# Who issues the paced loads of a backward pass: SyncE for all, or GpSimd for those of the filling products

## The chip, the cores and the metric

The kernel runs on one core of a Trainium2 chip. The metric is the device time of one execution in microseconds, the median over several runs. The core has five engines that run their own instruction streams and wait for each other through semaphores: PE (TensorE, matrix products into PSUM), ACT (ScalarE), DVE (VectorE), POOL (GpSimd) and SP (SyncE, which in this kernel only issues DMAs). PE's weight loads are shown as PEld. A DMA is issued by an instruction in the stream of one engine; an engine works through its stream in order, so a DMA behind a waiting instruction is issued late.

## The reference, cut to what matters

One transformer block in which attention and a gated feed-forward network stand side by side, and its gradients:

```python
def forward(x, wqkv, wo, w_gate, w_up, w_down):      # x: 1 x 2048 x 448, bf16
    xn = layernorm(x)
    q, k, v = split(xn @ wqkv)                         # 16 heads of 28
    p = softmax(q @ k.T * 28 ** -0.5)                  # 2048 x 2048 per head
    attn = (p @ v) @ wo
    ffn = (silu(xn @ w_gate) * (xn @ w_up)) @ w_down   # inner size 1792
    return x + attn + ffn

out, vjp = jax.vjp(forward, x, wqkv, wo, w_gate, w_up, w_down)
return out, *vjp(grad_out)
```

The kernel returns the output and six gradients.

## The kernel before, in words

Heads are worked on in 4 groups `g` of 4 heads. The first part computes the projections, the forward attention and the whole of the feed-forward network's inner work, and leaves in DRAM what the second part needs: queries with their gradients (`QD_d`), keys and values (`KD_d`), the inner activations and their gradients (`F_d`), the attention outputs (`OT_d`), transposed weights (`wT_d`, `wqc_d`).

The second part, the backward pass of attention, is one loop over 512 steps `k` (the constant `NB`), ordered group, head pair `hp`, key block `kc` of 512 keys, query block `qc`, query tile `qi` of 128. In the order of the code a step does the following.

- `row(k)`: PE computes the scores of two heads (line 845) and, for the step before, the gradients of the probabilities (line 853).
- `ew(k)`: ACT takes the exponentials (line 870, tile `e_sb`); DVE multiplies them with the gradients (line 878). The result `ds` goes to a tile `ds_sb` for query tiles 0 to 2 and to `ds_pe` for tile 3.
- For query tiles 0 to 2 of each block `b` of four steps, `dst_dma` lets SP issue a DMA transpose of `ds` into the tile `dsT` (line 863); for tile 3, and for tile 2 of a few blocks, PE transposes and ACT copies (`tr_unit`, lines 938 and 943).
- `kv(k)`: PE sums the gradients of keys and values (lines 956 and 960).
- `dq_unit(b)` comes in step `4 * b + 13`: PE multiplies the `dsT` of the block's four tiles with the keys (line 987), ACT writes the scaled result to `dq_st` (line 1000), which has a single buffer, and POOL adds it to `dq_acc` (line 1002), or for the last key block writes the sum to `dqT` (line 1004).

PE, ACT and DVE keep this order. What is left of PE's time is given to filling products, in pieces, within the steps: `y_unit` (the output, from `h_c`, `o_c`, `x_c`, `wd_e`, `wd_sb`, `wo_sb`; line 1111), `dx_unit` (the feed-forward part of the input's gradient, from `dau_c` and `wguT`; line 1167) and `dc_unit` (the attention part, from `dc` and `wqT`; line 1214), with smaller ones between them. Their order is a list; what each gets in a step is a time budget in the code.

Their operands come from DRAM by paced loads. `drip` puts a load on the list `slow`, sorted by the step in which it is due. In each step `drop` computes a rate that has every load on the list issued three steps before it is due, adds it to a credit, and issues loads from the head of the list while the credit is positive (line 802). `have` issues at once what a unit is about to need and what is still on the list. The keys `kd` and queries `qd` of the next group come by the same list (`load_k`, `load_q`). All of these loads are issued by SP, in the order of the code, between the transposes of `ds`. Results are stored through `store`, which holds each back two steps and then lets POOL issue it (line 835).

Of the kernel before, what the change touches and what calls it, by code (L numbers as in the profile page):

```python
# [105 lines left out]
def kernel(  # L106
# [23 lines left out]
    PE, DVE, ACTE, POOL, SP = nc.tensor, nc.vector, nc.scalar, nc.gpsimd, nc.sync  # L130
# [6 lines left out]
    QD_d = dram.tile([G, 4, P, 4, 512], BF16)  # L137
    KD_d = dram.tile([G, 4, P, 3, 512], BF16)
# [436 lines left out]
    for i in range(len(chain) + LEAD):  # L575
# [4 lines left out]
        k = i - LEAD  # L580
# [102 lines left out]
    for t in range(4):  # L683
        run(T_unit(xnT, xn_t, t, t % 2 == 0, ps_s if t < 2 else None))
    DVE.tensor_reduce(out=r_ones[:],
                      in_=ident_f[:].rearrange("p (a b) -> p a b", b=HP)[:, :, 28:30],
# [11 lines left out]
    for c in range(3):  # L698
        k = 4 * c
        t = 4 * c + 4  # L700
# [37 lines left out]
    def new_q(g, qc):  # L738
        qside[g, qc] = kq.tile([P, 4, 512], BF16, name="qd", bufs=6)
        return qside[g, qc]  # L740

    def new_k(g, kc):
        kside[g, kc] = kq.tile([P, 3, 512], BF16, name="kd", bufs=5)
        return kside[g, kc]
# [29 lines left out]
    slow = []  # L774
    RATE = 100 << 10
    now = 0

    def drip(key, pieces, due):
        slow.extend((due, key, o, i) for o, i in pieces)
        slow.sort(key=lambda x: x[0])  # L780
# [3 lines left out]
    def size(o):  # L784
        nb = 2 if o.dtype == BF16 else 4
        for x in o.shape:
            nb *= x
        return nb

    def drop():  # L790
        nonlocal credit
        if not slow:
            credit = 0
            return
        rate, cum = RATE, 0
        for due, _, o, _ in slow:
            cum += size(o)
            rate = max(rate, (cum - credit) / max(due - now - 3, 1))
        credit += rate
        while slow and credit > 0:  # L800
            _, _, o, i = slow.pop(0)
            SP.dma_start(out=o, in_=i)
            credit -= size(o)

    def have(*keys):
        for x in [x for x in slow if x[1] in keys]:
            slow.remove(x)
            SP.dma_start(out=x[2], in_=x[3])

    def load_q(g, qc):  # L810
        t = new_q(g, qc)
        drip(("q", g, qc), [(t[:], QD_d[g, qc])], 128 * g + 4 * qc - 4)

    def load_k(g, kc):
        t = new_k(g, kc)
        drip(("k", g, kc), [(t[:], KD_d[g, kc])], 128 * g + 16 * kc - 4)

    steps = [(g, hp, kc, qc, qi) for g in range(G) for hp in range(2) for kc in range(4)
             for qc in range(4) for qi in range(4)]
    NB = len(steps)  # L820
# [16 lines left out]
    def row(k):  # L837

        if k < NB:
            g, hp, kc, qc, qi = steps[k]  # L840
            have(("q", g, qc), ("k", g, kc))
            for j in range(2):
                s_ps = ps_b.tile([P, 512], FP32, name="sb", bufs=3)
                r = HP * (2 * hp + j)
                PE.matmul(s_ps[:], lhsT=qside[g, qc][r:r + HP, 0, qi * P:(qi + 1) * P],  # L845
                          rhs=kside[g, kc][r:r + HP, 0, :], start=True, stop=True, tile_position=(r, 0))
                sps[k, j] = s_ps
        if 1 <= k <= NB:
            g, hp, kc, qc, qi = steps[k - 1]
            for j in range(2):  # L850
                d_ps = ps_b.tile([P, 512], FP32, name="db", bufs=3)
                r = HP * pv(2 * hp + j)
                PE.matmul(d_ps[:], lhsT=qside[g, qc][r:r + HP, 1, qi * P:(qi + 1) * P],  # L853
                          rhs=kside[g, kc][r:r + HP, 1, :], start=True, stop=True, tile_position=(r, 0))
                dps[k - 1, j] = d_ps
# [35 lines left out]
    k = 0  # L891
# [200 lines left out]
    load_y(0, 0)  # L1092
    drip(("y", 0, 0), [(wo_sb[:], wo_d[:])], 36)
    load_k(0, 2)
    drip(("y", 0, 1), [(wdp[1][:, a:b, :], wd_v[:, NH + a:NH + b, :]) for a, b in ((0, 4), (4, 7))], 50)

    load_y(0, 1)
    load_k(0, 3)

    def y_unit(ch, half, ti):  # L1100
        if ti == 0:
            have(("y", ch, half))
            nxt = 2 * ch + half + 2
            if nxt < 8:
                load_y(nxt // 2, nxt % 2)
        tsl = slice(ti * P, (ti + 1) * P)
        mm = [(ych[ch, half][:, i, tsl], wdp[half][:, i, :]) for i in range(NH)]
        mm += [(ych[ch, 3 + half][:, i, tsl], wo_sb[:, 2 * half + i, :]) for i in range(2)]
        ps = ps_g.tile([P, 512], FP32, name="genb")
        for i, (l, r) in enumerate(mm):  # L1110
            PE.matmul(ps[:, :D], lhsT=l, rhs=r, start=(i == 0), stop=(i == len(mm) - 1))
            if i < len(mm) - 1:
                yield 189
        if half == 0:
            yts[ti] = yp.tile([P, D], FP32, name="yt", bufs=5)
            DVE.tensor_tensor(out=yts[ti][:], in0=ps[:, :D], in1=ych[ch, 2][:, ti, :], op=ALU.add)
        else:
            y = yp.tile([P, D], BF16, name="y")
            DVE.tensor_tensor(out=y[:], in0=ps[:, :D], in1=yts[ti][:], op=ALU.add)
            store(out0_d[:, 4 * ch + ti, :], y[:])  # L1120
        yield 189
# [33 lines left out]
    def dx_unit(ch, fq, ti):  # L1155
        if ti == 0:
            have(("dx", ch, fq))
            nxt = 4 * fq + ch + 1
            if nxt < 12:
                load_dx(nxt % 4, nxt // 4)  # L1160
        d = dxs[ch, fq]
        f0, f1 = FQ[fq]
        n = 2 * (f1 - f0)
        tsl = slice(ti * P, (ti + 1) * P)
        ps = ps_g.tile([P, 512], FP32, name="genb")
        for i in range(n):
            PE.matmul(ps[:, :D], lhsT=d[:, i // 2, i % 2, tsl], rhs=dxs["w", fq][:, i // 2, i % 2, :],  # L1167
                      start=(i == 0), stop=(i == n - 1))
            if i < n - 1:
                yield 189  # L1170
        o = dxs["g"][:, 4 * ch + ti, :]
        if fq == 0:
            ACTE.copy(out=o, in_=ps[:, :D])
        else:
            DVE.tensor_tensor(out=o, in0=ps[:, :D], in1=o, op=ALU.add)
        yield 189
# [178 lines left out]
    for k in range(NB + 12):  # L1355
        now = k
        if k < NB:
            g, hp, kc, qc, qi = steps[k]
            if hp == 1 and kc > 0 and qc == 2 and qi == 2 and g + 1 < G:
                load_k(g + 1, kc - 1)  # L1360
            if g > 0 and hp == 0 and kc == 0 and qc == 2 and qi == 2:
                load_k(g, 3)
            if hp == 1 and g + 1 < G and qi == 3 and (kc, qc) in NEXT:
                load_q(g + 1, NEXT.index((kc, qc)))
        m = k % 4
        if k <= NB:
            if k >= K0:
                row(k)
                ew(k)
            flush(k)  # L1370
            if 2 <= k:
                drop()
# [89 lines left out]
```

## Time and profile before

| | us |
|---|---|
| median of 3 runs | 1411.97 |
| lowest and highest run | 1410.12, 1415.71 |
| the profiled execution: time | 1411.65 |
| the profiled execution: span, first to last instruction | 1409.9 |
| busy: PE, ACT, DVE, POOL | 1322.0, 1213.3, 1148.3, 411.9 |
| mean granted TensorE clock | 0.981 of full |

The profile is one execution. Busy time of an engine is the union of its instructions; SP has no busy time in it, since issuing is not counted, but its instructions have start and duration in the timeline. "Idle before" is the time that an engine stood still before an instruction, with the instruction or DMA that ended it. The first exponential of the loop of 512 steps starts at 604.1 us and the last step's at 1361, so that a step takes 1.48 us on average and a block of four steps 5.9 us.

### The profile page before, as it was taken

The numbers are of one execution on the slowest core, as the hardware profiler recorded it, in microseconds if no ns is written. First come the engines' busy times: TensorE is split into PE (matmuls) and PEld (weight loads), VectorE is DVE, ScalarE is ACT, GpSimd is POOL, SyncE is SP. The second block draws the span as 40 slices with busy tenths as digits, with TensorE's granted clock in tenths as the row PEclk, the third lists the DMA queues.
The fourth block names the chain that finished last, engine by engine and source line by source line (L and its number), as shares of the span: only waits on it lengthen the run. The fifth ranks groups of instructions, "written<-read, shape, count | busy, mean of one in ns | idle before, by whom it ended". The sixth has DMA issues, their size and how long they took to land. (4 is left out here: it accounts for less than half of the span.)

```text
span 1409.9 us, 34764 instructions
## 1 busy us (share of the span) xinstructions
PE 1322.0 (94%) x12697; PEld 561.2 (40%) x12758; DVE 1148.3 (81%) x2001; ACT 1213.3 (86%) x2199; POOL 411.9 (29%) x577
## 2 busy tenths in 40 slices
PE   5889999989999999988999999999999999999985
PEld 2333333333333333333434444444444444444442
DVE  6577756666666677677989989988899999999988
ACT  5789998989999999867988889899989898888964
POOL 6574534464334444311121111301211112020105
PEclk9899999999999999989999999999999999999998
DMA  6697967876677677699999999999999999999972
GB/s 157 160 206 167 236 138 167 199 157 165 151 193 175 162 168 162 174 234 213 213 223 222 229 222 184 213 222 230 244 170 201 215 218 238 183 182 197 207 144 61
DMA packets 672205, 267.88 MB, mean 190 GB/s; under 512 B 597914, under 2 KB 646546, under 8 KB 672034
## 3 DMA queue, kind: packets, MB, share of 16 engines
q1 hardware_dynamic: 663586, 252.42, 87.9%
q0 software_dynamic: 7040, 12.93, 3.7%
q8 instruction: 100, 1.64, 0.5%
q14 instruction: 71, 0.58, 0.1%
q10 hardware_dynamic: 1408, 0.30, 0.1%
HBM read 64.37 MB, written 59.62 MB: 88 GB/s over the span
## 5 line engine op out<-in xcount | busy, mean ns | idle before, releaser
L870 ACT ACTIVATE e_sb<-sb 128x512 bf16<-128x512 f32 x1024 | 541.1, 606 | 31.4 <-PE db L853 28.3
L878 DVE TENSOR_TENSOR ds_sb<-db,e_sb 128x512 bf16<-128x512 f32 x770 | 483.2, 682 | 33.0 <-issue 9.0
L639 ACT ACTIVATE eT<-s_w 128x1024 bf16<-128x1024 f32 x256 | 264.5, 1033 | 56.0 <-PE s_ps L636 53.7
L641 ACT ACTIVATE eT<-s_ps 128x512 bf16<-128x512 f32 x512 | 286.7, 612 | 0.0
L845 PE MATMUL sb<-kd,qd 32*128 32x512 bf16 x1024 | 234.2, 385 | 5.7 <-DMA kd<-KD_d 2.0
L853 PE MATMUL db<-kd,qd 32*128 32x512 bf16 x1024 | 234.5, 386 | 4.4 <-DVE ds_sb L878 3.7
L1002 POOL TENSOR_TENSOR dq_acc<-dq_acc,dq_st 128x256 f32<-128x256 f32 x64 | 46.2, 723 | 485.2 <-ACT dq_st L1000 485.2
L878 DVE TENSOR_TENSOR ds_pe<-db,e_sb 128x512 bf16<-128x512 f32 x254 | 163.4, 685 | 21.1 <-PE db L853 13.2
L404 POOL TENSOR_TENSOR nn<-nn,ag 128x512 f32<-128x512 f32 x56 | 71.4, 1274 | 242.8 <-DVE ag L402 234.2
L956 PE MATMUL acc<-e_sb,qd 128*32 128x512 bf16 x1024 | 135.6, 387 | 0.0
L636 PE MATMUL s_ps<-QQ,KK 32*128 32x512 bf16 x512 | 120.1, 387 | 2.2
L1167 PE MATMUL genb<-wguT,dau_c 128*128 128x448 bf16 x448 | 109.7, 356 | 0.0
L960 PE MATMUL acc<-ds_sb,qd 128*32 128x512 bf16 x770 | 107.7, 388 | 0.0
L636 PE MATMUL s_w<-QQ,KK 32*128 32x512 bf16 x512 | 100.7, 390 | 3.8 <-ACT eT L639 1.2
L845 PEld LDWEIGHTS <-qd 32*128 32x128 bf16 x1024 | 48.4, 91 | 133.8 <-issue 114.6
L445 PE MATMUL gen<-xn_t,f_sp 128*128 128x448 bf16 x416 | 91.8, 354 | 3.4 <-DVE nn L419 1.9
L943 ACT COPY dsT<-sb 128x512 f32<-128x512 f32 x137 | 79.9, 590 | 16.3 <-PE sb L938 8.2
L445 PEld LDWEIGHTS <-f_sp 128*128 128x128 bf16 x640 | 55.8, 98 | 79.5 <-issue 34.2
L987 PE MATMUL sb<-dsT,kd 128*32 128x256 bf16 x2048 | 79.0, 274 | 6.8 <-DMA dsT<-ds_sb 6.1
L938 PE MATMUL sb<-ident_bf,ds_pe 128*128 128x128 bf16 x1016 | 77.6, 219 | 1.1 <-DVE dsT L941 0.8
L938 PEld LDWEIGHTS <-ds_pe 128*128 128x128 bf16 x1016 | 66.3, 98 | 24.2 <-issue 7.4
L405 POOL TENSOR_TENSOR nn<-nn,tt 128x512 f32<-128x512 f32 x56 | 72.5, 1295 | 4.4
(183 smaller groups left out, 2044.3 us busy)
## 6 DMA issues: line engine op xcount, KB each, us to landing
F_d<-hda SPq DMA_DIRECT2D x56, 384.0 KB
dau_c<-F_d SPq DMA_DIRECT2D x24, 512.0 KB
qd<-QD_d SPq DMA_DIRECT2D x16, 512.0 KB
kd<-KD_d SPq DMA_DIRECT2D x16, 384.0 KB
dsT<-ds_sb SPq DMA_TRANSPOSE x374
h_c<-F_d SPq DMA_DIRECT2D x8, 512.0 KB
wT_d<-wT_f SPq DMA_DIRECT2D x14, 256.0 KB
KD_d<-qk_sp SPq DMA_DIRECT2D x7, 512.0 KB
```

What stands on the lines that cost most here:

```text
L445: PE.matmul(ps[:, :D], lhsT=fsp[fc][:, t // 4, w, t % 4, :], rhs=rhs[:, t, :], start=(t == 0), stop=(t == NT - 1))
L636: PE.matmul(sp4[hh], lhsT=KK[g][r:r + HP, kt * P:(kt + 1) * P], rhs=QQ[g][r:r + HP, qsl], start=True, stop=True, tile_position=(r, 0))
L639: ACTE.activation(out=e2[0][:], in_=wide[:], func=ACT.Exp, scale=SCALE)
L641: ACTE.activation(out=e2[1][:, j], in_=sp4[2 + j], func=ACT.Exp, scale=SCALE)
L845: PE.matmul(s_ps[:], lhsT=qside[g, qc][r:r + HP, 0, qi * P:(qi + 1) * P], rhs=kside[g, kc][r:r + HP, 0, :], start=True, stop=True, tile_po ...
L853: PE.matmul(d_ps[:], lhsT=qside[g, qc][r:r + HP, 1, qi * P:(qi + 1) * P], rhs=kside[g, kc][r:r + HP, 1, :], start=True, stop=True, tile_po ...
L870: ACTE.activation(out=est[k][:, j], in_=sps.pop((k, j))[:], func=ACT.Exp, scale=SCALE)
L878: DVE.tensor_tensor(out=ds[:, j], in0=dps.pop((k - 1, j))[:], in1=est[k - 1][:, j], op=ALU.mult)
L938: PE.transpose(ps[:, c, :], ds[:, c // 4, (c % 4) * P:(c % 4 + 1) * P], ident_bf[:])
L956: PE.matmul(a[r:r + HP, :], lhsT=sp4[:, 1, r:r + HP], rhs=e[:, j, :], start=first, stop=last, tile_position=(0, r), skip_group_check=True)
L960: PE.matmul(a[r:r + HP, :], lhsT=sp4[:, 0, r:r + HP], rhs=ds[:, j, :], start=first, stop=last, tile_position=(0, r), skip_group_check=True)
L1167: PE.matmul(ps[:, :D], lhsT=d[:, i // 2, i % 2, tsl], rhs=dxs["w", fq][:, i // 2, i % 2, :], start=(i == 0), stop=(i == n - 1))
```

## The change

In the loop of 512 steps, POOL issues the paced loads that feed the filling products. SP keeps the loads of keys and queries, and everything that is issued after the last step (`now >= NB`). Keys and queries are put on the list as due eight steps before their first use, where it was four. The list, its pacing and the loads themselves stay.

```diff
+    def by(key):
+        return SP if key[0] in "qk" or now >= NB else POOL
+
     def drop():
...
         while slow and credit > 0:
-            _, _, o, i = slow.pop(0)
-            SP.dma_start(out=o, in_=i)
+            _, key, o, i = slow.pop(0)
+            by(key).dma_start(out=o, in_=i)
             credit -= size(o)
 
     def have(*keys):
         for x in [x for x in slow if x[1] in keys]:
             slow.remove(x)
-            SP.dma_start(out=x[2], in_=x[3])
+            by(x[1]).dma_start(out=x[2], in_=x[3])
 
     def load_q(g, qc):
         t = new_q(g, qc)
-        drip(("q", g, qc), [(t[:], QD_d[g, qc])], 128 * g + 4 * qc - 4)
+        drip(("q", g, qc), [(t[:], QD_d[g, qc])], 128 * g + 4 * qc - 8)
 
     def load_k(g, kc):
         t = new_k(g, kc)
-        drip(("k", g, kc), [(t[:], KD_d[g, kc])], 128 * g + 16 * kc - 4)
+        drip(("k", g, kc), [(t[:], KD_d[g, kc])], 128 * g + 16 * kc - 8)
```

## The prediction

> **What bounds the kernel now.** The first view is the busy time by stretch, cut at the places where the filling products change. Its columns are time, busy time and instructions of PE, PEld, DVE, ACT, POOL, then the granted clock, the DMA share and GB/s.
>
> ```profile
> 616.00:671.00 55.00, 50.89 (x524) 22.05 (x519) 43.95 (x73) 43.40 (x88) 6.51 (x11) 0.86 1.15 219
> 671.00:840.00 169.00, 162.20 (x1871) 70.94 (x1869) 155.67 (x256) 145.81 (x292) 30.51 (x49) 0.99 1.16 220
> 840.00:1240.00 400.00, 398.38 (x4630) 181.75 (x4630) 374.34 (x633) 358.65 (x724) 62.83 (x96) 1.00 1.10 210
> ```
>
> From 840 us on PE is busy 99.6% of the time: nothing that concerns loads is to be had there. Before it, PE stands still for 4.1 + 6.8 = 10.9 us. The waits of PE after 600 us say for what:
>
> ```profile
> PE sb L987 <- DMA dsT<-ds_sb: 6.1, 7, 2.1
> PE sb L845 <- DMA kd<-KD_d: 2.0, 1, 2.0
> ```
>
> So 8.1 us are waits for a transposed `ds` or for keys. The timeline of the longest shows why the transpose was late; first DVE, then the other engines:
>
> ```profile
> 709.32 1.27 DVE L878 TENSOR_TENSOR ds_sb<-db,e_sb 128x512 bf16<-128x512 f32 x2
> ```
>
> ```profile
> 717.54 0.57 SPq L802 DMA_DIRECT2D h_c<-F_d  x1
> 718.21 7.84 SPq L863 DMA_TRANSPOSE dsT<-ds_sb  x4
> ...
> 721.13 2.54 POOL L835 DMA_DIRECT2D dqkvc_d<-dqT  x4
> ...
> 726.09 0.67 SPq L802 DMA_DIRECT2D h_c<-F_d  x1
> 726.48 0.75 PE L987 MATMUL sb<-dsT,kd 128*32 128x256 bf16 x16 [2.06 <-DMA dsT<-ds_sb]
> ```
>
> The product ready at 709.32 + 1.27 = 710.6 us is transposed by the second of the four, which SP starts at 719.5 us: 8.9 us late. It lands at 726.3 us and PE goes on at 726.5. SP's rows stand end to end here. Pairing all transposes with their products in order, they start 7 to 10 us late from 616 to 825 us, and mostly 0 to 4 us late afterwards. From product to use there are 15.9 us in this case, 2.06 of them the stall; a transpose takes 4.5 us to land (median, 640 to 738 us). The lag starts to cost at 15.9 - 2.1 - 4.5 = 9 us, just where it stands.
>
> SP's budget says why. In 671 to 840 us there are 28 blocks of four steps, 6.0 us each. SP's 82 transposes take 136.7 us (1.67 each) and its 31 loads 21.7 us (0.70 each). A block holds 3 transposes and 1.1 loads: 5.0 + 0.8 us, and four gaps of 0.07: 6.1 us. SP is full and sets the pace; PE alone needs 5.7 us (steps 80 to 128, 68.2 us for 12 blocks).
>
> **The change, part by part.** The prices of issuing, as minimum/median/maximum in ns, from SP's loads and transposes and from POOL's DMAs:
>
> ```profile
> L802 SPq DMA_DIRECT2D dau_c<-F_d x32: 360/575/1996, 889.9 to 1203.2; - x32
> L802 SPq DMA_DIRECT2D h_c<-F_d x16: 572/582/1447, 635.9 to 833.8; - x16
> ```
>
> ```profile
> L863 SPq DMA_TRANSPOSE dsT<-ds_sb x374: 1231/1305/4052, 616.5 to 1361.8; - x187
> ```
>
> ```profile
> L835 POOL DMA_DIRECT2D out_dram<-y x16: 557/560/593, 696.8 to 877.3; - x16
> ```
>
> ```profile
> L360 POOL DMA_DIRECT2D w_f<-in_B_w_gate_dram x14: 822/825/1030, 12.2 to 532.4; - x14
> ```
>
> *Taken from SP:* 95 of the 121 paced loads (32 `dau_c`, 16 `h_c`, 12 `dc`, 8 `o_c`, 8 `wguT`, 19 others); 26 of keys and queries stay. Of the 31 loads in 671 to 840 us 25 go. A block then costs SP 3 x 1.67 + 0.2 x 0.70 + 0.2 = 5.4 us with the transposes as slow as now, and 3 x 1.31 + 0.4 = 4.3 us at their median, both under 5.7. The lag shrinks by 0.3 to 1.4 us a block and is under 9 us soon after the turn at 616 us. What is late next is nothing of SP: the 5.7 us of PE.
>
> *Given to POOL:* a store of 128 pieces takes 0.56 us, a load of 384 pieces 0.83, so 1 ns a piece: 0.95 us for an `h_c` of 512 pieces, 0.69 for a `dau_c` of 256, some 0.75 on average, 95 x 0.75 = 71 us. They lie in POOL's idle time: it waits 485 us before its 64 `dq_acc` additions and 110 us before its 24 of `dqT`. The single `dq_st` lets ACT write the next only when POOL has read the last, once a block; POOL's block is an addition of 0.72, a store of 0.56 and one load, at most two: 2.2 to 3.2 us of 5.7. So it costs nothing; if that cover were gone, ACT, and behind it the exponentials and PE, would wait for all above 5.7.
>
> *New waits on POOL:* a load waits for the products that last read its buffer. These stand before it in PE's order, and both engines are at about the same step, so additions and stores queued behind it lose little; bound 0 to one step (1.5 us) in a block that has 2.5 us to spare: nothing. The first loads (`h_c`, `x_c`, `o_c`, `wo_sb`) share POOL with four pairs of stores that wait for DVE until 656 us; by the code the last load before the first `y_unit` is in step 25, behind the third pair at 643.8 us, and SP issued it at 657.1. That is earlier than now.
>
> *Landing:* the loads run on the same DMA engines as before. POOL's stores land in 2.5 to 6.4 us, SP's loads in 3.2 to 5.5 between 640 and 738 us; filling products have no wait of note for a load today (0.3 us for `o_c`), though SP is 7 to 10 us late, and that reserve stays.
>
> *Due eight ahead:* following the list in the code, the keys that made PE wait 2.0 us (group 1, block 1) go out in step 134 now (SP issues them at 821.1 us) and in step 117 after; used in step 144. Some `h_c` loads go nine steps later in exchange, 12 or more steps before they are due. The buffers that early keys and queries fill are free by then. The 2.0 us go.
>
> *Clock:* the granted clock is 0.50 from 726.8 to 730.2 us, right after the gap of 2.06: 1.7 us of work lost, which I count. It is also halved from 662.0 to 668.8 us, beginning before the gap at 664.4: not counted, up to 3.4 us more if the lag is its cause.
>
> Sum: 6.1 + 2.0 + 1.7 = 9.8 us. As a check by steps: the four steps that hold the longest waits took 5.33, 4.38, 3.77 and 3.99 us where their like take 1.9, 2.0, 2.0 and 1.9: 9.7 us. The upper end: all idle time of PE before 840 us above the 0.4% of later, 10.0 us, plus the clock's 1.7 + 3.4: 15. The profiled execution took 1411.65 us, 0.3 under the median, so 1411.97 - 9.8 = 1402.2 us. What a measurement of this kernel can tell from no change is about 0.5%, 7 us: the limits are 1404.9 and 1419.
>
> SP's time being short in the budget above, a rule speaks against the change. The Trainium skill (DMA: Bandwidth & Descriptors, section "Issuing engines are not separate DMA queues") has all DMAs end on the same 16 engines, and several issuers save only the sequencer's time, "usually small relative to the DMA itself". By the rule alone the gain is 0 and the time 1412; by the row of 7.84 us for four transposes issued end to end it is the sequencer that is short.
>
> **The rivals.**
>
> *The transposes stay slow, no gain to speak of.* Issuing takes 1.23 us when the queue is empty, more when the engines are behind, and the bytes do not change. If each takes 1.85 to 1.95 us, a block is 5.7 to 6.05 us for SP and the lag stays. For it: 1.96 us each in the 7.84 above, with POOL storing beside them. Against: the mean of 1.67 already holds today's loads in the same queue. Time 1405 to 1412.
>
> *The loads on POOL's queue slow the transposes: slower.* Place: 616 to 840 us, where a load or store of POOL would run beside most transposes; price: the one begun at 719.53 beside POOL's stores took 2.18 us; with that everywhere SP needs 3 x 2.2 + 0.35 = 6.95 us a block, 0.95 over today's 6.0, in 28 blocks 27 us; with two in three beside a load 3 x 1.88 + 0.35 = 6.0, nothing. It decides from 1.9 us a transpose on. I take the middle, 1425. The same page's section "Queues, rings and completion order" has an engine alternate between queues packet by packet, which would let a load's larger packets in between a transpose's; it gives no price for that.
>
> *POOL holds its additions up: slower too.* If a load kept POOL until it lands (4.5 us) instead of 0.95, a block with two loads would need 0.7 + 0.6 + 9 = 10.3 us, 4.6 too many, some 20 blocks: up to 92 us. Against: POOL issues four stores in 2.54 us without waiting for the landings. 1425 to 1450.
>
> **How the numbers follow.** Forecast 0.58 (1397 to 1405, near 1402); slow transposes 0.24 (1405 to 1412); slowed by POOL's queue 0.11; POOL holding 0.07. Of the last two 0.15 lies above 1419. Faster 0.58, same 0.24 + 0.03 = 0.27, slower 0.15. The range from 1398 to 1416 leaves out 0.02 below and 0.16 above.
>
> **What would show it.** Right: transposes of `ds` issued less than 4 us after their product from 650 us on, the wait of line 987 for `dsT` and of line 845 for `kd` under 1 us each, no halved clock at 727 us, blocks of 5.7 us before 840. Wrong: a mean issue of a transpose over 1.85 us before 840, ACT idle before `dq_st` with POOL as its cause, `dq_acc` additions starting over 2 us after `dq_st`, filling products waiting for `h_c` or `dau_c`, or the gaps gone while 840 to 1240 us got longer.

## The result, and the profile after

The changed kernel took 1462.92 us (median of 6 runs, 1455.45 to 1477.31), beside 1413.84 for the kernel before (6 runs, 1407.95 to 1416.27): ratio 1.0344, interval 1.03 to 1.0388. It is 49 us slower; the forecast was 10 us faster. The profiled execution, 1477.31 us with a span of 1475.5, is the longest of the six and is left out of the ratio; where a size matters, the runs below stand beside it. Line numbers of the changed kernel are higher by 3 (987 is 990, 863 is 866, 835 is 838, 1002 is 1005).

First the busy time by stretch, with the columns as in the prediction:

```profile
616.00:671.00 55.00, 50.81 (x532) 22.80 (x533) 44.35 (x74) 43.56 (x88) 11.68 (x19) 0.88 1.14 228
671.00:840.00 169.00, 142.78 (x1602) 62.63 (x1598) 135.12 (x221) 125.11 (x249) 39.97 (x62) 0.91 1.15 193
840.00:1240.00 400.00, 378.13 (x4299) 170.54 (x4291) 347.99 (x587) 335.92 (x676) 88.82 (x135) 0.97 1.13 195
```

PE stands still for 26.2 us in the second row, where it was 6.8, and for 21.9 us in the third, where it was 1.6. DVE and ACT do less in these rows too, the granted clock is lower (0.91 and 0.97 for 0.99 and 1.00), and the GB/s fell from 220 and 210 to 193 and 195. So the loss is not in one place: it runs on from 671 us. The waits of PE after 600 us say for what:

```profile
PE sb L990 <- DMA dsT<-ds_sb: 60.9, 19, 8.5
PE sb L848 <- DMA qd<-QD_d: 0.7, 1, 0.7
```

The wait for keys is gone, as forecast. The wait for a transposed `ds` did not go from 6.1 us to nothing but to 60.9 (48.2 in the run "Issuer alone" below, profiled at 1470 us). Over the whole span PE's idle time grew by 50.4 us (span less busy, 138.3 for 87.9) and its busy time by 15.2 (1337.2 for 1322.0, with a mean clock of 0.963 for 0.981): together the 65.6 us between the two spans.

Why the transposes are late is seen in the timeline around the longest stall, which ends at 724.7 us; first SP, then POOL, then PE:

```profile
707.88 19.74 SPq L866 DMA_TRANSPOSE dsT<-ds_sb  x7
```

```profile
702.20 0.55 POOL L805 DMA_DIRECT2D o_c<-OT_d  x1
702.74 0.76 POOL L805 DMA_DIRECT2D h_c<-F_d  x1
710.74 0.72 POOL L1007 TENSOR_TENSOR dqT<-dq_acc,dq_st 128x256 bf16<-128x256 f32 x1 [7.24 <-ACT dq_st L1003]
711.41 0.56 POOL L838 DMA_DIRECT2D out_dram<-y  x1
711.97 2.00 POOL L838 DMA_DIRECT2D dqkvc_d<-dkv  x4
```

```profile
724.72 1.04 PE L990 MATMUL sb<-dsT,kd 128*32 128x256 bf16 x16 [8.45 <-DMA dsT<-ds_sb]
```

SP has no load in these 20 us, and yet seven transposes take 2.82 us each. The forecast freed SP of loads and found SP as full as before, with slower transposes. At 813.83 us the same row reads `27.29` for six, 4.5 us each. All 374, as minimum/median/maximum in ns:

```profile
L866 SPq DMA_TRANSPOSE dsT<-ds_sb x374: 1231/1337/10762, 615.1 to 1427.5; - x187
```

The median hardly moved (it was 1305); the maximum went from 4052 to 10762. The loss sits in few, very slow transposes: 47 of the 374 took over 3 us, 5 in the kernel before. GpSimd's own prices, and what it waits for:

```profile
L805 POOL DMA_DIRECT2D dau_c<-F_d x32: 567/723/832, 909.4 to 1246.4; - x32
L805 POOL DMA_DIRECT2D h_c<-F_d x16: 751/762/918, 615.6 to 848.6; - x16
```

```profile
L1005 POOL TENSOR_TENSOR dq_acc<-dq_acc,dq_st 128x256 f32<-128x256 f32 x64 | 46.0, 718 | 422.9 <-ACT dq_st L1003 422.9
```

0.72 and 0.76 us a load, near the 0.75 of the prediction, and POOL still waits 422.9 us for ACT before its additions: it holds nobody up. The loads themselves land later than the 3.2 to 5.5 us that the prediction has for SP's, as the issues by kind show (last column, median us from issue to landing):

```profile
dau_c<-F_d POOLq DMA_DIRECT2D x24, 512.0 KB, 7.6
h_c<-F_d POOLq DMA_DIRECT2D x8, 512.0 KB, 8.1
```

### The profile page after: what moved, and what is told of

The parts are those of the page before. It is cut to its first block, busy times and chain, and to the rows that moved or that the text cites. A ratio compares the mean times of both kernels' runs of the same rounds, so it can differ in the third digit from the quotient of the medians.

```text
span 1475.5 us, 34789 instructions
## 1 busy us (share of the span) xinstructions
PE 1337.2 (91%) x12697; PEld 565.9 (38%) x12758; DVE 1149.3 (78%) x2001; ACT 1215.0 (82%) x2199; POOL 477.6 (32%) x672
## 5 line engine op out<-in xcount | busy, mean ns | idle before, releaser
L848 PE MATMUL sb<-kd,qd 32*128 32x512 bf16 x1024 | 237.8, 394 | 3.9 <-DMA qd<-QD_d 0.7
L1005 POOL TENSOR_TENSOR dq_acc<-dq_acc,dq_st 128x256 f32<-128x256 f32 x64 | 46.0, 718 | 422.9 <-ACT dq_st L1003 422.9
L990 PE MATMUL sb<-dsT,kd 128*32 128x256 bf16 x2048 | 83.5, 284 | 61.7 <-DMA dsT<-ds_sb 60.9
L1003 ACT ACTIVATE dq_st<-sb 128x256 f32<-128x256 f32 x88 | 33.7, 383 | 73.7 <-PE sb L990 73.7
L990 PEld LDWEIGHTS <-kd 128*32 128x32 bf16 x2048 | 55.3, 99 | 96.4 <-issue 54.4
```

The costliest lines, as they stand in the source:

```text
L990: PE.matmul(ps[r:r + HP, :256], lhsT=ks[:, kt, h:h + HP], rhs=t[:, par::2, j, kt, :], start=(kt == 0), stop=(kt == 3), tile_position=(0, r ...
```

## The experiments

My theory after the result: loads on GpSimd's software queue slow the DMA transposes, and PE waits for these. Its rivals: the due times, traffic with DRAM, the number or the size of the pieces, bursts, and a cost by another path than the transposes. Unless said otherwise the edit is to the changed kernel. "Wait for dsT" is PE's, after 600 us, from the profiled execution.

**Due times alone.** SP issues everything, as before; only the two due times stay changed.

```diff
-            by(key).dma_start(out=o, in_=i)               # in drop; in have the same
+            SP.dma_start(out=o, in_=i)
```

> SyncE issues every paced load as before; only keys and queries are due eight steps ahead. Theory A (the issuer costs the 49 us): 1405 to 1416 us, at most the 2.0 us wait for keys is gone, transposes still 7 to 10 us late before 840 us. Rival (the earlier keys and queries bunch the other loads, and this is what stalls): over 1430 us, with waits of the dq products for dsT of 15 us or more.

Measured: 1415.05 us, ratio 1.0003 (0.9981 to 1.0025); span 1410.9.

```profile
PE sb L987 <- DMA dsT<-ds_sb: 9.8, 7, 3.1
```

The wait for keys is gone here too, and worth nothing: the wait for `dsT` is 3.7 us longer than before in its place. The 2.0 us of the prediction were not to be had by themselves.

**Issuer alone.** GpSimd issues, due times of before.

```diff
-        drip(("k", g, kc), [(t[:], KD_d[g, kc])], 128 * g + 16 * kc - 8)
+        drip(("k", g, kc), [(t[:], KD_d[g, kc])], 128 * g + 16 * kc - 4)    # and so in load_q
```

> GpSimd issues the filling loads, keys and queries due four steps ahead as before. Theory A (the issuer costs it): 1450 to 1470 us, 40 to 60 us of waiting for dsT, and perhaps a few us for keys. Rival (the due time costs it): within 1395 to 1416 us.

Measured: 1466.17 us, ratio 1.0382 (1.0319 to 1.0445); wait for dsT 48.2. The issuer alone makes the loss.

**ScalarE as the issuer.** The same 95 loads on ACT's queue, which the profile calls hardware like SP's; GpSimd's is software.

```diff
-        return SP if key[0] in "qk" or now >= NB else POOL
+        return SP if key[0] in "qk" or now >= NB else ACTE
```

> ScalarE issues the 95 filling loads, so that they run on a second hardware queue instead of GpSimd's software queue. Theory S (GpSimd's queue, with its packets of 4 KB, is what slows the transposes): the mean issue of a ds transpose back at 1.7 us or less, waits for dsT under 10 us; ScalarE loses 95 x 0.58 us of its own time, some of it on the path: 1405 to 1450 us. Rival Q (any second queue beside the transposes does it): mean issue over 1.9 us in the stretches with loads, waits for dsT of 30 us or more, 1460 us or longer.

Measured: 1420.97 us, ratio 1.0046 (1.0007 to 1.0086). Its PE waits:

```profile
PE sb L848 <- ACT dsT L946: 8.5, 5, 5.9
PE sb L848 <- ACT e_sb L873: 6.3, 4, 3.1
PE sb L990 <- DMA dsT<-ds_sb: 4.7, 4, 2.2
```

The wait for `dsT` is a tenth of that with GpSimd. What is lost instead is lost behind ACT, whose stream now holds the loads. A second queue as such is not the 49 us; GpSimd's is. It is not free for the transposes, though: their mean issue did not go back to 1.7 us, as theory S had it, but to 1.84 us in 616 to 840 us and 1.76 in 840 to 1240 (kernel before 1.68 and 1.57, changed kernel 2.10 and 1.96). A PE that waits for ACT also asks for `dsT` later, which may hide some of the lateness.

**Source in SBUF.** GpSimd's loads read a tile in SBUF in place of DRAM; the data that the filling products get is not theirs.

```diff
-            by(key).dma_start(out=o, in_=i)
+            by(key).dma_start(out=o, in_=src(key, o, i))   # a slice of xn_t
```

> GpSimd issues the filling loads with the same sizes and destinations, but they read from a tile in SBUF instead of DRAM, so the filling products get other data. Theory M (the read from DRAM holds the DMA engines while transposes wait behind it): the waits for dsT fall under 15 us and the time to 1400 to 1420 us. Rival Q/S (the packets of the second queue do it, wherever they read): waits for dsT of 40 us or more, 1445 us or longer.

Measured: 1460.86 us (two runs), ratio 1.0336 (1.0283 to 1.0389).

```profile
PE sb L1003 <- DMA dsT<-ds_sb: 48.5, 19, 7.6
```

The traffic with DRAM is not the cause.

**Smaller DMAs.** GpSimd issues each load as single rows of 0.9 to 1 KB a partition, then as pairs of rows.

```diff
-            by(key).dma_start(out=o, in_=i)
+            for a in range(o.shape[1]):
+                for b in range(o.shape[2]):            # where o has four dimensions
+                    by(key).dma_start(out=o[:, a, b], in_=i[:, a, b])
...                                                    # pairs: two rows in each DMA
```

> The changed kernel, but each filling load that GpSimd issues is cut along its free dimensions into pieces of one row of 896 or 1024 B a partition, each a DMA of its own; bytes, order and due times stay. In the changed kernel the packets of the software queue are 3.5 to 4.4 KB where SP's were 0.9 to 2 KB. Theory P (size of packet: the DMA engines serve the two queues packet by packet, so that one large packet holds up one 256-byte packet of a transpose for 160 ns and more): packets of 1 KB take a quarter of that, the time falls to that of the loads on ScalarE's queue or little more, 1418 to 1432 us, with waits for dsT before the dq matmuls of 10 to 20 us in place of 61. Theory N (cost of each DMA of the software queue: its descriptors, some three times as many DMAs): the waits grow, 1475 to 1540 us. Theory B (bytes on a second queue, whatever their form): unchanged, 1455 to 1472 us.

> As the run with pieces of one row, but two rows of 896 or 1024 B (some 2 KB a partition) go in one DMA. Theory P: between that run and the changed kernel, 1432 to 1450 us. Theory N: a little above the changed kernel, 1465 to 1490 us. Theory B: unchanged, 1455 to 1472 us.

Measured: single rows 1472.15 us, ratio 1.0396 (1.0345 to 1.0446), wait for dsT 61.8; pairs of rows between 1452.36 and 1500.13 in four runs, too far apart for a verdict (the profiled one, at 1452.36, waits 40.5 us for `dsT`). My first theory P can't be judged by these: in the trace some three quarters of the software queue's bytes go in packets of 4096 B all the same (7888 of them with single rows, 7792 in the changed kernel), so one packet holds several rows whatever the cut. Theory N had 1475 us or more and is not borne out: three times the number of load issues after 625 us (285 for 92) cost no more than the spread.

**Part of the loads.** GpSimd issues only the loads of the y products (before 840 us), then only the others.

```diff
-        return SP if key[0] in "qk" or now >= NB else POOL
+        return SP if key[0] != "y" or now >= NB else POOL     # others: key[0] in "qky"
```

> The changed kernel, but GpSimd issues only the loads for the forward's y and output products (h_c, x_c, o_c, wd, wo, about 13 of 37 MB, all of them before 840 us); the loads of dau_c, wguT, dc and the rest stay with SP. If the loss of 49 us goes with the bytes on the software queue, a third of it is left: 1427 to 1434 us. If it stands in the stretch in which SP is behind (616 to 840 us), as my rival had it, nearly all is left: 1445 to 1460. If freeing SP there is worth the 8 us of the forecast and the queue costs little by these loads, 1405 to 1412.

> The other part: GpSimd issues only the loads after 840 us (dau_c, wguT, dc and the tail's, about 24 of 37 MB), SP those of the y products. By bytes: two thirds of the loss, 1443 to 1450 us. By the stretch in which SP is behind: little of the loss, 1414 to 1422 us.

Measured: y loads 1431.86 us, ratio 1.0108 (1.0063 to 1.0153); the others 1459.05, ratio 1.0321 (1.0254 to 1.0387). The waits, of each:

```profile
PE sb L990 <- DMA dsT<-ds_sb: 24.7, 7, 7.6
```

```profile
PE sb L990 <- DMA dsT<-ds_sb: 37.7, 19, 8.4
```

Both parts lose, the second more. Worked out over the rows of the trace, a transpose took on the mean, in 616 to 840 and in 840 to 1240 us: kernel before 1.68 and 1.57 us; y loads on GpSimd 2.11 and 1.63; the others 1.71 and 1.97; the changed kernel 2.10 and 1.96. The transposes slow down just where GpSimd's loads run, in either stretch. By bytes (13 of 37 MB) the y loads were forecast at 1427 to 1434 and hit; the others came out above their 1450, so the loss is not strictly in proportion.

**Packets of 4 KB on ScalarE's queue.** The run with the source in SBUF, issued by ACT (the data is again not the products' own). Rows are contiguous at both ends there.

```diff
-        return SP if key[0] in "qk" or now >= NB else POOL
+        return SP if key[0] in "qk" or now >= NB else ACTE
```

> The run with the loads' source in SBUF (xn_t in place of the DRAM tensors, so the output products are of the wrong data), but issued by ScalarE and not by GpSimd: the same bytes by the same rows of up to 4 KB that are contiguous at both ends, on a hardware queue. The cut into rows did not change the packets of the software queue (still 4096 B), so size of packet and kind of queue are still one. Theory P (size of packet): if its packets are as large as the software queue's, the loss is the software queue's, 1445 to 1465 us with some 45 us of waits for dsT. Theory K (kind of queue): as the loads on ScalarE's queue before, 1415 to 1428 us, with under 10 us of waits for dsT.

Measured: 1436.3 us, ratio 1.0149 (1.0108 to 1.019): between the two expectations. Its packets became larger, if not quite as large as the software queue's (4096 of 4 KB, 229 ns each on the mean, and nearly all the rest of its 36.7 MB in packets of 1.8 to 3.6 KB; 263 ns for those of 4 KB of the software queue in the changed kernel). The waits:

```profile
PE sb L861 <- ACT e_sb L886: 13.2, 7, 7.3
PE sb L861 <- ACT dsT L959: 11.0, 7, 5.0
PE sb L1003 <- DMA dsT<-ds_sb: 3.3, 3, 2.0
```

The wait for `dsT` is 3.3 us where the same loads on GpSimd's queue had 48.5, and the whole loss is 21 us where it was 46. So large packets alone are not the whole cause, and the change from GpSimd's queue to ACT's takes off more than half. But the transposes themselves are nearly as slow: 1.93 and 1.82 us on the mean before and after 840 us, where GpSimd's queue with the same source had 2.01 and 1.91, and ACT's with small packets 1.84 and 1.76. The transposes that took over 4 us are fewer (10 for 20), and PE waits for ACT in place of `dsT`. So a part for the size of the packets is not excluded.

**y loads on ScalarE's queue.** This tests the step on SP's time: 33 loads fewer for SP before 840 us, by a queue that costs little.

```diff
-        return SP if key[0] in "qk" or now >= NB else POOL
+        return SP if key[0] != "y" or now >= NB else ACTE
```

> The y products' loads alone (33 DMAs before 840 us) issued by ScalarE, all others by SP, queries and keys due eight steps ahead. It frees SP where the forecast saw it full, by a queue that costs the transposes little, and leaves ScalarE 33 x 0.37 us = 12 us of issues. If SP's load issues are what makes the transposes late in 616 to 840 us, the 6 to 10 us of waits for dsT go and the time is 1404 to 1410 us; if the transposes are late by their own issue time (1.5 to 2 us each), 1412 to 1418 us.

Measured: 1412.01 us, ratio 0.9998 (0.9968 to 1.0029); wait for dsT 4.1, once. No gain. A transpose took 1.91 us in 616 to 840 us, where it was 1.68: three times the 0.23 is 0.69 us a block, and the loads that left SP were 0.9 x 0.70 = 0.63. Yet the lag shrank as forecast: paired with their products, the transposes start 3.4 us late between 616 and 825 us (median), 8.2 in the kernel before. The wait for `dsT` fell from the 9.8 us of due times alone, and waits for ACT took most of that back (5.2 us between 616 and 840 us, 0.9 with due times alone). The same y loads on GpSimd's queue made 2.11 us a transpose and 24.7 us of waits.

**The stores off the software queue.** From the kernel with due times alone: the 79 stores on SP, then on ACT.

```diff
-        held.append((now + 2, o, i))
+        held.append((now + 4, o, i))
...
-            (POOL if now < NB else SP).dma_start(out=o, in_=i)
+            SP.dma_start(out=o, in_=i)                            # or ACTE before NB
```

> The kernel before with queries and keys due eight steps ahead, and the 79 stores of the backward (dkv, dqT, y, dwq; 7 MB) issued by SP in place of GpSimd, held two steps longer: no software queue is left beside the transposes. By the slope of the runs so far (kernel before 7.1 MB on the software queue after 616 us and a span of 1411 us, y loads alone 20.5 MB and 1434, the others alone 31.0 and 1454: 1.8 us a MB), taking 7 MB away gains up to 12 us: 1400 to 1408. If the loss begins only where the software queue runs for long, no gain; and if SP's additional 79 x 0.65 = 51 us of issues make it late, 1414 to 1425.

> As the run with the stores on SP, but ScalarE issues them (79 x 0.35 = 28 us of its time). By the slope 1400 to 1408 us; if ScalarE's issues hold up its evictions as the 95 loads did (15 us of PE waits), 1408 to 1416 us.

Measured: SP 1438.24 us, ratio 1.0157 (1.0137 to 1.0177); ACT 1467.18, ratio 1.0358 (1.0326 to 1.0391). Both missed. They say little of the queue, since a store waits in the order of the engine that issues it. With SP, PE waits 18.2 us for DVE's `ds_sb` and 4.8 for `dsT`; with ACT, 25.9 for `dq_st` and 11.6 for `dq_acc`. Whether the 7 MB of stores cost the kernel before anything stays open; with them on SP, a transpose took 1.51 us in 616 to 840 us, with due times alone 1.71, but in a slower loop.

**Single pieces dripped.** Each load enters the list as its single rows, so that GpSimd should issue them apart (keys, queries and loads of one row stay whole).

```diff
-        slow.extend((due, key, o, i) for o, i in pieces)
+        slow.extend((due, key, o[:, c], i[:, c]) for o, i in pieces for c in range(o.shape[1]))
```

> The changed kernel, but each filling load enters the list of due loads as its single rows (64 to 256 KB in place of 256 to 512 KB), so that GpSimd issues them one by one between the steps and not in bursts. Theory B (bytes on the software queue count): 1450 to 1475 us, and some 45 us a DMA engine in packets of the software queue that take over 0.8 us, as in the changed kernel. Theory U (bursts: the transposes starve while the second queue moves over 200 GB/s): 1420 to 1440 us.

Measured: 1465.64 us, ratio 1.0321 (1.0252 to 1.0389); wait for dsT 53.2. The loss is there as before, but this does not test the bursts: 143 of the 217 loads after 625 us are issued within 1 us of the one before them, and the software queue moves over 200 GB/s in 65 bins of 1 us, 67 in the changed kernel. Theory U is not settled.

**Copies in place of transposes.** With GpSimd's loads, and with SP's (due times of the change in both):

```diff
-        SP.dma_start_transpose(out=dsT[b][:, qi].rearrange("p j kt s -> p (j kt) s"),
+        SP.dma_start(out=dsT[b][:, qi].rearrange("p j kt s -> p (j kt s)"),
...
```

> The changed kernel with each DMA transpose of ds (dsT from ds_sb, 1024 bf16 a partition) replaced by a plain DMA copy of the same bytes on the same queue with the same waits; the transposition is left out, so dq is of the wrong data. Theory T (GpSimd's loads cost time only because the transposes, at 1.5 us of the DMA engines for 256 KB in 256-byte packets, leave no room): the copies are short, the waits of the dq matmuls for dsT go, and the time is that of the run with copies and SP's loads within 8 us, 1390 to 1412. Theory G (the software queue costs by another path, such as GpSimd's issues): 30 us or more above that run.

> The kernel before with queries and keys due eight steps ahead, all loads by SP, and the same plain copies in place of the transposes: the reference for the run with GpSimd's loads. Transposes that are never late are worth the 8 us of the forecast: 1400 to 1408 us; if something else binds as closely, 1408 to 1416.

> The run with plain copies for the transposes (the transposition is left out) and GpSimd's loads, once more, with more rounds, beside the one with SP's loads on the same chip. If freeing SP is worth something where the transposes are not late, 1394 to 1397 us and 3 us or more under the other; if not, within 2 us of it.

> The run with plain copies (the transposition is left out) and SP's loads, once more: 1397 to 1401 us if the first pair held, 1395 to 1398 if its difference was noise.

Measured with GpSimd's loads: 1395.37 us, ratio 0.9858 (0.9825 to 0.9892), and again 1397.38, 0.9884 (0.9862 to 0.9906). With SP's: 1399.17, 0.9889 (0.986 to 0.9918), and again 1397.29, 0.9894 (0.9876 to 0.9913). The two kernels can't be told apart. The waits of PE for `dsT`, and a copy's issue in 671 to 840 us, both with GpSimd's loads (first run):

```profile
PE sb L990 <- DMA dsT<-ds_sb: 1.4, 1, 1.4
```

```profile
L866 SPq DMA_DIRECT2D dsT<-ds_sb x86: 464/465/845, 671.5 to 839.9; - x86
```

The same loads, on the same software queue, with the same issues on GpSimd, cost nothing once the transposes are gone. This is the run that settles the path: in this kernel GpSimd's loads cost PE time only through the DMA transposes beside them. It also bounds what relief of the transposes can bring: 1.1%, some 15 us.

## Why the prediction was wrong

*Landing: the step that failed.* "The loads run on the same DMA engines as before" was written down as a cost of nothing. What was looked at there is when the loads land, not what they do to the transposes, and so the sum went by "the transposes as slow as now", 1.67 us each. In the changed kernel a transpose took 2.10 us in 616 to 840 us and 1.96 in 840 to 1240, and the wait for `dsT` that the sum took as gone grew from 6.1 to 60.9 us. The loads do run on the same engines, but in a queue of their own they no longer take turns with the transposes in SP's order. In the changed kernel, counting packets in bins of 1 us from 620 us on, the 256-byte packets of the transposes move 164 GB/s while the software queue is silent, 87 while it moves 1 to 100 GB/s, and 30 while it moves over 200. In the middle case all queues together move 144 GB/s, less than the 187 without it. That the engines lose time, and don't only share it, is suggested by this and not shown: what is asked of the engines differs from bin to bin, and in the kernel before, where the software queue has the stores alone, the same two kinds of bin move 211 and 206 GB/s.

*SP's budget: a price that was not fixed.* "5.4 us with the transposes as slow as now" took 1.67 us as a price of SP. It rose to 1.91 with a hardware queue beside it and to 2.10 with the software queue. That SP's loads add to the lag was right: with the y loads on ACT it fell to 3.4 us, though no time came of it. What was at stake was read rightly too: with copies steps 16 to 176 took 227 to 230 us in place of 241, 5.7 us a block, which is the prediction's figure for PE alone. But with copies, at 0.46 us each for SP, who issues the loads makes no difference. So the gain was to be had from cheaper transposes; no change of the loads' issuer tried here brought it. A row of SP full end to end could not tell whether the sequencer or the DMA engines filled it. The first rival's sum has a slip: 3 x 1.85 to 3 x 1.95 and the budget's 0.34 make 5.9 to 6.2 us a block, not 5.7 to 6.05.

*The rule weighed.* The Trainium skill (DMA: Bandwidth & Descriptors, section "Issuing engines are not separate DMA queues") has several issuers save the sequencer's time and nothing more. It was right against my gain; the 3.4% lost shows that the issuer does more than it says.

*The rival that held.* Loads on POOL's queue slow the transposes: right mechanism, 0.11 of the chance, 1425 us for 1463. Its price for 616 to 840 us was fair, taken at 13 us and bounded at 27: y loads alone cost 15 us by the ratio (24.3 by the profiled span, 1434.2 for 1409.9, the longest of four runs). Its place was wrong. I had set 840 to 1240 us aside since PE was busy 99.6% and nothing was to be had there; there was much to be lost. A transpose of 1.97 us makes 3 x 1.97 = 5.9 us a block before any load of keys, over the 5.84 that a block took there before; the other loads alone made the span 44.4 us longer. The sign named for this rival came true, a mean issue over 1.85 us before 840. A range that gave the rival its whole loop would have reached past 1460.

*POOL and its additions:* hidden, as predicted. The 0.75 us a load came out on the average by luck: at 1 ns a piece `h_c` was put at 0.95 us and took 0.76, `dau_c` at 0.69 and took 0.72. *Keys and queries:* the wait went, and gave nothing. *Clock:* 1.7 us were to be gained by a clock that stays whole; its mean fell from 0.981 to 0.963.

*What stays open:* why GpSimd's software queue disturbs more than ACT's hardware one, and what part the size of the packets and the bursts have in it. A trail: summed per DMA engine, from 620 us to 10 us before the end of the dq products, the packets of over 0.8 us on GpSimd's and ACT's queues take

| kernel | us an engine | span above before, us |
|---|---|---|
| before | 2.0 | 0 |
| y loads on ACT | 7.3 | 0.1 |
| all loads on ACT | 16.9 | 17.2 |
| y loads on GpSimd | 21.7 | 24.3 |
| all loads on ACT, source in SBUF | 24.8 | 30.0 |
| other loads on GpSimd | 35.2 | 44.4 |
| GpSimd, source in SBUF | 47.0 | 47.0 |
| changed kernel | 44.7 | 65.6 |

The two grow together, roughly, but with copies 25.9 us an engine cost nothing, and what makes a packet long no run here shows.

## What to carry to other kernels

Before moving DMAs to another engine's queue, look at what shares the DMA engines with them: here a stream of transposes that PE waits for was slowed by both second queues tried, by ACT's (from 1.68 to 1.84 us each before 840 us) and more by GpSimd's (to 2.10). An issuing engine that is full end to end may be waiting for the DMA engines and not be short of time; taking some of its DMAs off it, and seeing whether the rest get longer, is a test. Replacing them by cheaper ones of the same bytes bounds what can be won, but frees the engine and the DMA engines at once. A stretch in which the bounding engine is busy 99.6% has next to nothing to win, but a change that touches it can lose there, so a rival is priced over the whole of its reach.

## What was unexpected

- In the changed kernel all queues together moved 144 GB/s in the bins in which the software queue moved 1 to 100 GB/s, and 187 where it was silent; with the stores alone on it, in the kernel before, nothing of the kind (211 and 206).
- With DRAM as the source, most bytes of GpSimd's loads go in packets of 4096 B whatever the rows of the DMA; with the same loads on SP's and ACT's queues nearly all packets are one row (896 to 2048 B).
- A DMA transpose of 256 KB kept SP for 1.23 us at the least, a copy of the same bytes for 0.46, and with copies the kernel was 1.1% faster. Summed over its packets, a transpose took 1.66 us of each DMA engine (kernel before), a copy 0.71 (GpSimd's loads). The Trainium skill (Advanced Engine Details and Errata, section "X-Bar Transpose (TRN2)") has transposes as fast as regular DMAs; in these runs they are not.
